# Seven-product matmuls with a 192-row first half: where the 64 leftover rows go

## The chip, the cores and the metric

The kernel runs on one core of a Trainium2 chip. The metric is the device time of one launch in microseconds (us); lower is better. A core has a matrix engine (PE, with its weight loads shown apart as PEld), a vector engine (DVE), a scalar engine (ACT), GpSimd (POOL) and SyncE (SP). Each engine works through its own queue in order. PE writes to PSUM, in banks of 512 float32 columns; DVE and ACT read it there. DMAs are issued from the queues of SP, POOL and ACT.

## The reference: two attention and two gated layers over 2048 tokens

The input is 2048 tokens of 448 features, in float32. The same two blocks are applied twice, with the same weights:

```python
x = x + attention(layernorm(x), wqkv, wo)      # 16 heads of 28
x = x + gated(layernorm(x), w_gate, w_up, w_down)
x = x + attention(layernorm(x), wqkv, wo)
x = x + gated(layernorm(x), w_gate, w_up, w_down)
# gated(z) = (sigmoid(z @ w_gate) * (z @ w_up)) @ w_down, inner size 1792
```

Gate, up, query, key and value products all sum over the 448 features. That sum is what the change rearranges: 448 is three times 128 and 64 more.

## The kernel before: seven products in place of eight, in float16 parts

**Number format.** A float32 operand is held as two float16 parts, high and low, with value = high + low. A product takes three matmuls: high x high, high weights x low input, low weights x high input. For the last 64 feature rows, two of these share one matmul of 128 rows: the lower 64 rows of an operand hold the part that the second product needs.

**Seven products.** Gate and up (from block to block of 512 tokens), and query and key in layer 1, are made two output tiles of 128 columns at a time. The features are cut into two halves, the tokens of a block into two halves of 256, and the output into the two tiles, so that one 2x2 by 2x2 block product of this kind would need eight products. The kernel uses a scheme with seven, on sums and differences of the halves. The first half of the features has 256 rows, the second 192 (128 and 64). Of the seven products, four (`k` = 0 to 3, input tile `wide`) involve 256 rows: two groups of 128 rows with three matmuls each, six matmuls. Three (`k` = 4 to 6, input tile `short`) involve 192 rows: three matmuls for the full group and two for the 64 rows, five matmuls. All are in `of_halves`, line 636 of the profile.

**Weights.** The sums and differences of the weights do not depend on the tokens. They are made once, during the attention of layer 0, by `Prepare`: its steps are tied to the key blocks that PE has mixed, one split of a tile pair about every nine key blocks. POOL's queue reads the raw weights ahead and writes the results back (lines 1365, 1367, 1388); DVE forms four sums (line 260), the high halves (line 266) and the low halves (line 269, `low` in `split_sums`). A pair's result has 25 groups of 128 columns (`N_SUMS`) and goes to DRAM. There are 14 gate and up splits and 3 for query and key. In the gated layers a pair's two tiles (gate and up) are loaded from there two pairs ahead, through POOL's queue (line 1744).

**Attention of layer 0.** For each head, PE makes scores in groups of three tiles (line 1503), ACT takes their exponentials (line 1518), PE mixes the values with them (line 1554). Two score tiles of most heads go aside: DVE makes their exponentials by a polynomial (lines 1528 to 1537). The aside scores go to the PSUM bank in which the head before was accumulated; DVE's transposition (line 1583, in `finish`) frees it. So DVE's queue holds, in program order: polynomial, the end of each head, and the splits of `Prepare`.

**Inputs.** `Block.half_steps` makes `wide` and `short` for a block of tokens, one step after another between the products of the block before: DVE subtracts, ACT writes the high halves (line 458), DVE the low ones (line 467). `raw` holds the features of a block as four groups; the fourth has only 64 rows, and its lower 64 rows are zeroed by POOL (line 477 in step `r11`). Three `double` copies and one copy of the remainder by ACT (lines 471 and 523) fill the lower 64 rows of `short` in the last steps.

**One pair of the gated stage.** `gate_and_up` issues for gate and up in turn: `first`, `apart`, `second`, `third` (the `wide` products), `c11_c22`, `c21`, `c12` (the `short` ones). `first`, `second` and `third` accumulate in one bank, which ACT copies out after each (line 1936), before the next may write it; DVE adds the side bank (lines 1952, 1959). From block 1 on, pieces of the down product of the block before stand between them (line 1863).

Of the kernel before, what the change touches and what calls it, by code (L numbers as in the profile page):

```python
# [19 lines left out]
P = 128  # L20
# [36 lines left out]
N_SUMS = 25  # L57
# [5 lines left out]
SHORT = ((10, 23, 12), (11, 24, 13), (8, 22, 9))  # L63
# [61 lines left out]
def interleaved_layers(ctx: ExitStack, tc: tile.TileContext, x_in, wqkv, wo, w_gate, w_up,  # L125
# [137 lines left out]
    def split_sums(t, v, by):  # L263
# [13 lines left out]
        for to, hi, a in ((t[:, 14:16], t[:, 0:2], v[:, 0:2, 0]),  # L277
                          (t[:, 16:20], t[:, 2:6], s12),
                          (t[:, 20:23], t[:, 6:9], s34[:, 0:3]),
                          (t[:, 23:25], t[:, 10:12], v[:, 2])):  # L280
            low(to, hi, a)
        low(t[64:P, 9], t[0:64, 9], s34[0:64, 3])
        low(t[64:P, 12:14], t[0:64, 12:14], v[0:64, 3])
# [23 lines left out]
    class Block:  # L307
# [91 lines left out]
        def gather(self):  # L399
            rows = self.scr.rearrange("j r i n -> (j r) (i n)")  # L400
            self.raw = big.get("xraw", [P, 4, W])
            nc.sync.dma_start(self.raw[:, 0:3, :],
                              rows[0:384].rearrange("(k p) n -> p k n", p=P))
            nc.sync.dma_start(self.raw[0:64, 3, :], rows[384:D])
# [25 lines left out]
        def half_steps(self):  # L430
# [38 lines left out]
            def double(to):  # L469

                nc.scalar.copy(to[64:P, 0, 1], to[0:64, 0, 1])


            def r11():
                self.wide = big.get("xwide", [P, 4, 2, 2, W // 2], F16)
                if not self.turned:
                    nc.gpsimd.memset(self.raw[64:P, 3, :], 0.0)
# [8 lines left out]
            def t2():  # L486
                low(self.wide[:, 1], self.t1)
                self.t3 = subtract("t3", cut(2, 2), cut(0, 2))
                high(self.wide[:, 2], self.t2)
                qrt.put(self.t1)  # L490

            def t3():
                low(self.wide[:, 2], self.t2)
                self.t4 = subtract("t4", cut(2, 0), self.t2)
                high(self.wide[:, 3], self.t3)
                qrt.put(self.t2)

            def r21():
                self.short = big.get("xshort", [P, 4 if self.whole else 3, 2, 2, W // 2], F16)
                low(self.wide[:, 3], self.t3)  # L500
                high(self.short[:, 0], cut(2, 0))
                qrt.put(self.t3)

            def t4():
                low(self.short[:, 0], cut(2, 0))
                high(self.short[:, 1], self.t4)

            def r22():
                low(self.short[:, 1], self.t4)
                double(self.short[:, 0])  # L510
# [7 lines left out]
            def last_low():  # L518
# [4 lines left out]
                nc.scalar.copy(self.short[64:P, 1, 1, 1], self.raw[64:P, 3, 0:W // 2])  # L523
                double(self.short[:, 1])
                big.put(self.raw)

            def last_rows():
                double(self.short[:, 2])
# [39 lines left out]
        def turn_raw(self):  # L568
# [3 lines left out]
            nc.gpsimd.memset(self.raw[64:P, 3, :], 0.0)  # L572
            for j in range(TB):
                self.turn(j)
            for kt, pt in self.pt.items():
                n = P if kt < 3 else 64
                nc.scalar.copy(self.raw[0:n, kt, :], pt[0:n])
# [45 lines left out]
    def of_halves(pm, w, blk, k, first):  # L623


        if k < 4:
            x = blk.wide[:, k]
            terms = [(w[:, i], x[:, j, t]) for t in range(2)
                     for i, j in ((2 * k + t, 0), (2 * k + t, 1), (14 + 2 * k + t, 0))]
# [1605 lines left out]
```

## Time and profile before

| what | value |
|---|---|
| median of 3 runs | 1886.36 us (1886.18 to 1886.47) |
| span of the profiled execution | 1884.5 us |
| end-to-end time of that execution | not listed apart; its span is 1.9 us below the median |
| first attention, exponentials of layer 0 | from about 120 to 560 us |
| gated stage of layer 0 | 599 to 952 us |
| query, key and value products of layer 1 | 952 to 1040 us |
| gated stage of layer 1 | 1528 to 1881 us |
| granted PE clock | 1.00 |
| DMA | 275.82 MB, mean 146 GB/s |

A row of the groups names the line, the engine, the operation and the tiles (result <- inputs), the shape, how often it ran, and its time. In a row in order of time, the first number is the start in us from the span's begin, the second the length; a bracket tells how long the engine was idle before it and what released it. A row that stands for several instructions ends in x and their count, and its length goes from the first start to the last end.

### The profile page before, as it was taken

What the parts mean: (1) busy time and instruction counts of PE and PEld (TensorE: products, weight loads), DVE (VectorE), ACT (ScalarE), POOL (GpSimd) and SP (SyncE); (2) the same over time, 40 slices, a digit from 0 to 9 for tenths busy, and PEclk for the clock granted to TensorE, in tenths of its full rate; (3) what the DMA queues carried; (4) which work ended last, traced back from release to release, by engine and by line L of the source; (5) the groups of instructions that cost most, each with busy time, mean ns of one, the idle gap of its engine ahead of it and who ended that gap; (6) DMA issues with size and microseconds to landing.
All of it is one profiled execution on the core that took longest, in us unless ns stands there. A gap on an engine that the chain in (4) does not pass through costs nothing. (4 is left out here: it accounts for less than half of the span.)

```text
span 1884.5 us, 57358 instructions
## 1 busy us (share of the span) xinstructions
PE 1875.9 (100%) x24609; PEld 1385.2 (74%) x24609; DVE 1489.2 (79%) x3018; ACT 1424.8 (76%) x1897; POOL 233.1 (12%) x458
## 2 busy tenths in 40 slices
PE   9999999999999999999999999999999999999999
PEld 4455555555566899999987566777876568999998
DVE  7758999998997887788877587787778689877664
ACT  6569999999993655555568899999999757555541
POOL 3001112222202111111110000000000021111110
PEclk9999999999999999999999999999999999999999
DMA  7674454454333755646763322122121246566553
GB/s 257 183 216 126 132 159 125 129 149 119 124 107 88 267 199 212 221 189 247 235 170 99 91 52 52 29 51 52 32 47 32 72 163 230 198 228 224 203 206 142
DMA packets 116005, 275.82 MB, mean 146 GB/s; under 512 B 14174, under 2 KB 72014, under 8 KB 115616
## 3 DMA queue, kind: packets, MB, share of 16 engines
q0 software_dynamic: 31952, 163.16, 24.1%
q1 hardware_dynamic: 82640, 107.55, 20.2%
q8 instruction: 195, 3.19, 0.7%
q10 hardware_dynamic: 1152, 1.38, 0.3%
q14 instruction: 66, 0.54, 0.1%
HBM read 210.57 MB, written 53.08 MB: 140 GB/s over the span
## 5 line engine op out<-in xcount | busy, mean ns | idle before, releaser
L1518 ACT ACTIVATE prob_s<-sc 128x1536 f32<-128x1536 f32 (+1 forms) x657 | 887.9, 1486 | 6.6 <-PE sc L1503 3.4
L1554 PE MATMUL acc<-prob_s,val_s 128*32 128x256 f32 (+3 forms) x7708 | 577.3, 383 | 0.0
L1503 PE MATMUL sc<-qp_s 114*32 114x512 f16 x7868 | 560.9, 379 | 0.0
L636 PEld LDWEIGHTS <-gu_s 128*128 128x128 f16 x4368 | 426.7, 98 | 45.9 <-PE op L1683 0.7
L1503 PEld LDWEIGHTS <-qp_s 114*32 114x32 f16 x8192 | 289.6, 96 | 187.9 <-issue 81.9
L1554 PEld LDWEIGHTS acc<-prob_s,val_s 128*32 128x32 f32 x7708 | 290.3, 110 | 125.9 <-issue 11.7
L636 PE MATMUL chain<-xwide_s,gu_s 128*128 128x256 f16 x2016 | 247.5, 273 | 0.0
L1863 PE MATMUL dnp<-dn_s,hparts_s 128*128 128x224 f16 x2184 | 245.9, 259 | 0.0
L1863 PEld LDWEIGHTS <-hparts_s 128*128 128x128 f16 x2184 | 210.2, 98 | 5.1
L1534 DVE SCALAR_TENSOR_TENSOR power_q<-power_q,expo_q 128x512 f32<-128x512 f32 x243 | 168.2, 692 | 8.3
L1936 ACT COPY one_q<-chain 128x256 f32<-128x256 f32 x224 | 82.3, 372 | 114.3 <-PE chain L636 113.8
L1952 DVE TENSOR_TENSOR one_q<-side,one_q 128x512 f32<-128x512 f32 x112 | 72.1, 686 | 97.7 <-PE side L636 97.5
L636 PE MATMUL side<-xshort_s,gu_s 128*128 128x256 f16 x1120 | 140.6, 273 | 0.0
L1744 POOL DMA_DIRECT2D gu_s<-gu_parts x104 | 55.9, 538 | 438.7 <-PE side L636 435.5
L1816 ACT CAST hparts_s<-hsums_q 128x256 f16<-128x256 f32 (+1 forms) x152 | 71.5, 485 | 35.8 <-DVE hsums_q L1828 23.4
L1554 PE MATMUL acc<-power_q,val_s 128*32 128x256 f32 (+3 forms) x300 | 94.2, 396 | 0.0
L636 PE MATMUL side<-xwide_s,gu_s 128*128 128x256 f16 x672 | 91.7, 273 | 0.0
L1583 DVE STREAM_TRANSPOSE oturned_q<-acc 128x512 f32<-128x512 f32 x32 | 22.9, 717 | 82.5 <-PE acc L1554 82.2
L1963 ACT ACTIVATE one_q<-one_q 128x512 f32<-128x512 f32 x56 | 35.3, 630 | 65.0 <-DVE one_q L1952 64.7
L1820 DVE TENSOR_TENSOR hparts_s<-hsums_q,hparts_s 128x256 f16<-128x256 f32 (+1 forms) x152 | 72.8, 517 | 5.7 <-ACT hparts_s L1816 5.7
L1528 DVE TENSOR_SCALAR expo_q<-aside,base 128x512 f32<-128x512 f32 x81 | 60.6, 748 | 21.0 <-PE aside L1503 20.6
L621 PE MATMUL qkp<-xhl_s,wqk_s 128*128 128x512 f16 x308 | 69.6, 379 | 0.9 <-ACT wqk_s L241 0.6
(258 smaller groups left out, 2410.2 us busy)
## 6 DMA issues: line engine op xcount, KB each, us to landing
gu_s<-gu_parts POOLq DMA_DIRECT2D x104, 800.0 KB, 5.9
dn_s<-dn_parts POOLq DMA_DIRECT2D x42, 784.0 KB, 7.5
qp_s<-qk_scr SPq DMA_DIRECT2D x96, 224.0 KB
gu_parts<-pack_s POOLq DMA_DIRECT2D x14, 800.0 KB, 3.8
xt_scr<-xs_s SPq DMA_DIRECT2D x48, 224.0 KB
xraw_s<-xt_scr SPq DMA_DIRECT2D x12, 768.0 KB
qk_scr<-qkhl_q SPq DMA_DIRECT2D x28, 256.0 KB
qp_s<-qk_scr SPq DMA_DIRECT2D x64, 112.0 KB
```

Source lines behind the costliest of these rows:

```text
L621: nc.tensor.matmul(pm, w, x, start=(i == 0), stop=(i == len(terms) - 1))
L636: nc.tensor.matmul(pm, a, x, start=(first and i == 0), stop=(i == len(terms) - 1), skip_group_check=True)
L1503: nc.tensor.matmul(ps[32 * j:32 * j + 32, :], hd.k[:, keys], hd.q[:, qb * W:(qb + 1) * W], start=True, stop=True, tile_position=(0, 32 * j))
L1518: nc.scalar.activation(prob[:, 0:n, :], ps[:, 0:n, :], AF.Exp, scale=exp_scale)
L1528: nc.vector.tensor_scalar(y, ps, base2[:, 0:1], -126.0, op0=ALU.mult, op1=ALU.max)
L1534: nc.vector.scalar_tensor_tensor(p, p, c[k], y, op0=ALU.add, op1=ALU.mult)
L1554: nc.tensor.matmul(acc[qb * VC:(qb + 1) * VC, s], v[:, kc % TB, h, :], probs[c * NB + qb][:, s], start=(kc == 0 and a == 0), stop=(kc == N ...
L1816: nc.scalar.copy(to[:, :, 0], a)
L1820: nc.vector.tensor_tensor(to[:, :, 1], a, to[:, :, 0], op=ALU.subtract)
L1863: nc.tensor.matmul(pm, a[:, x, t], w[:, p, y], start=(begin and n == 0 and (j == 0 or alone)), stop=(n == 2), skip_group_check=True)
L1936: nc.scalar.copy(to, pm)
L1952: nc.vector.tensor_tensor(one[m], side[m], one[m], op=ALU.add)
```

## The change: 192 rows first, and the 64 rows spread

The features change places: group 0 keeps rows 0 to 127, group 1 is now the 64 rows 384 to 447, groups 2 and 3 are rows 128 to 383 (`PLACES`). So the first half has 192 rows and the second 256. In the seven-product scheme the four `wide` products now have three matmuls for a full group and two for the 64 rows (`TAILS`), five matmuls; the three `short` products have two full groups, six matmuls.

Which lower rows hold what changes with it. `again` copies the high part of the 64 rows to the lower rows of the low part, in all four `wide` products (and, in layer 1, in the fourth `short` tile); `double` and the copy of the remainder go. In `last_rows`, DVE adds the lower rows of one `short` low part to those of another, and ACT copies them to the lower rows of the second `wide` tile. The zeroed lower rows are now in group 1.

The weights get 27 groups per pair. In `split_sums` the low halves are cut otherwise (five of 128 rows, three of 64 instead of four and two), POOL makes two copies, and DVE adds one group to another. POOL reads the raw weights in three DMAs per tile instead of two, and a block's `gather` on SP has three DMAs instead of two where the block is halved.

```diff
-N_SUMS = 25
+N_SUMS = 27
+PLACES = 0, 3, 1, 2
-SHORT = ((10, 23, 12), (11, 24, 13), (8, 22, 9))
+LOW_A = 14, 15, 16, 17
+TAILS = 1, 24, 25, 26
+SHORT = ((10, 12, 20, 22), (11, 13, 21, 23), (8, 9, 18, 19))
...
 # split_sums
-        for to, hi, a in ((t[:, 14:16], t[:, 0:2], v[:, 0:2, 0]),
-                          (t[:, 16:20], t[:, 2:6], s12),
-                          (t[:, 20:23], t[:, 6:9], s34[:, 0:3]),
-                          (t[:, 23:25], t[:, 10:12], v[:, 2])):
+        for to, hi, a in ((t[:, 14], t[:, 0], v[:, 0, 0]),
+                          (t[:, 15:17], t[:, 2:6:2], s12[:, 0:4:2]),
+                          (t[:, 17:19], t[:, 6:10:2], s34[:, 0:4:2]),
+                          (t[:, 19], t[:, 9], s34[:, 3]),
+                          (t[:, 20:24].rearrange("p (k z) n -> p k z n", k=2),
+                           t[:, 10:14].rearrange("p (k z) n -> p k z n", k=2), v[:, 2:4])):
             low(to, hi, a)
-        low(t[64:P, 9], t[0:64, 9], s34[0:64, 3])
-        low(t[64:P, 12:14], t[0:64, 12:14], v[0:64, 3])
+        low(t[64:P, 24:26], t[0:64, 3:6:2], s12[0:64, 1:4:2])
+        low(t[64:P, 26], t[0:64, 7], s34[0:64, 1])
+        low(t[64:P, 1], t[0:64, 1], v[0:64, 1, 0])
+        nc.gpsimd.tensor_copy(t[0:64, 24:27], t[0:64, 3:8:2])
+        nc.gpsimd.tensor_copy(t[64:P, 7], t[64:P, 23])
+        nc.vector.tensor_tensor(t[64:P, 19], t[64:P, 19], t[64:P, 23], op=ALU.add)
...
 # half_steps
-            def double(to):
-                nc.scalar.copy(to[64:P, 0, 1], to[0:64, 0, 1])
+            def again(to):
+                nc.scalar.copy(to[64:P, 1, 1], to[0:64, 0, 1])
             def r11():
                 self.wide = big.get("xwide", [P, 4, 2, 2, W // 2], F16)
                 if not self.turned:
-                    nc.gpsimd.memset(self.raw[64:P, 3, :], 0.0)
+                    nc.gpsimd.memset(self.raw[64:P, 1, :], 0.0)
                 self.t1 = subtract("t1", cut(0, 2), cut(0, 0))
                 high(self.wide[:, 0], cut(0, 0))
...
             def last_rows():
-                double(self.short[:, 2])
+                if self.whole:
+                    again(self.short[:, 3])
+                rows, lo = self.short[64:P, 1, 1, 1], self.short[64:P, 2, 1, 1]
+                nc.vector.tensor_tensor(rows, rows, lo, op=ALU.add)
+                nc.scalar.copy(self.wide[64:P, 1, 0, 1], lo)
...
 # of_halves
         if k < 4:
             x = blk.wide[:, k]
-            terms = [(w[:, i], x[:, j, t]) for t in range(2)
-                     for i, j in ((2 * k + t, 0), (2 * k + t, 1), (14 + 2 * k + t, 0))]
+            terms = [(w[:, 2 * k], x[:, 0, 0]), (w[:, 2 * k], x[:, 1, 0]),
+                     (w[:, LOW_A[k]], x[:, 0, 0]),
+                     (w[:, 2 * k + 1], x[:, 0, 1]), (w[:, TAILS[k]], x[:, 1, 1])]
         else:
             x = blk.short[:, k - 4]
-            main, low, tail = SHORT[k - 4]
-            terms = [(w[:, main], x[:, 0, 0]), (w[:, main], x[:, 1, 0]), (w[:, low], x[:, 0, 0]),
-                     (w[:, tail], x[:, 0, 1]), (w[:, tail], x[:, 1, 1])]
+            terms = [(w[:, SHORT[k - 4][i]], x[:, j, t])
+                     for t in range(2) for i, j in ((t, 0), (t, 1), (2 + t, 0))]
...
 # Prepare.read
-                    nc.gpsimd.dma_start(v[:, 0:3, z],
-                                        w[0:384, c].rearrange("(s p) n -> p s n", p=P))
-                    nc.gpsimd.dma_start(v[0:64, 3, z], w[384:448, c])
-                nc.gpsimd.memset(v[64:P, 3], 0.0)
+                    nc.gpsimd.dma_start(v[:, 0, z], w[0:P, c])
+                    nc.gpsimd.dma_start(v[:, 2:4, z],
+                                        w[P:384, c].rearrange("(s p) n -> p s n", p=P))
+                    nc.gpsimd.dma_start(v[0:64, 1, z], w[384:448, c])
+                nc.gpsimd.memset(v[64:P, 1], 0.0)
```

The products of the values, the lone query and key tile and the transposed copies follow the new places without a change of their count.

More of the change, by code (lines that the diff above doesn't have):

```diff
@@ L401, in gather @@
             self.raw = big.get("xraw", [P, 4, W])
-            nc.sync.dma_start(self.raw[:, 0:3, :],
-                              rows[0:384].rearrange("(k p) n -> p k n", p=P))
-            nc.sync.dma_start(self.raw[0:64, 3, :], rows[384:D])
+            tail = 1 if self.halves else 3
+            if self.halves:
+                nc.sync.dma_start(self.raw[:, 0, :], rows[0:P])
+                nc.sync.dma_start(self.raw[:, 2:4, :],
+                                  rows[P:384].rearrange("(k p) n -> p k n", p=P))
+            else:
+                nc.sync.dma_start(self.raw[:, 0:3, :],
+                                  rows[0:384].rearrange("(k p) n -> p k n", p=P))
+            nc.sync.dma_start(self.raw[0:64, tail, :], rows[384:D])
         def part(self, kt):
@@ L489, in t2 @@
                 high(self.wide[:, 2], self.t2)
+                again(self.wide[:, 0])
                 qrt.put(self.t1)
@@ L495, in t3 @@
                 high(self.wide[:, 3], self.t3)
+                again(self.wide[:, 1])
                 qrt.put(self.t2)
@@ L501, in r21 @@
                 high(self.short[:, 0], cut(2, 0))
+                again(self.wide[:, 2])
                 qrt.put(self.t3)
@@ L506, in t4 @@
                 high(self.short[:, 1], self.t4)
+                again(self.wide[:, 3])
             def r22():
                 low(self.short[:, 1], self.t4)
-                double(self.short[:, 0])
                 high(self.short[:, 2], cut(2, 2))
@@ L571, in turn_raw @@
             self.raw = big.get("xraw", [P, 4, W])
-            nc.gpsimd.memset(self.raw[64:P, 3, :], 0.0)
+            nc.gpsimd.memset(self.raw[64:P, 1, :], 0.0)
             for j in range(TB):
                 self.turn(j)
-            for kt, pt in self.pt.items():
+            for i, kt in enumerate(PLACES):
                 n = P if kt < 3 else 64
-                nc.scalar.copy(self.raw[0:n, kt, :], pt[0:n])
+                nc.scalar.copy(self.raw[0:n, i, :], self.pt[kt][0:n])
             big.put(self.xn)
```

20 lines of the change are left out of this document (9 added, 11 removed).

## The prediction

> **What bounds the kernel now.** I read the page first, then the busy time by stretch, the products' line, the order in time inside one pair, and the waits. On the page TensorE (PE) is busy all the way and nothing else is:
>
> ```profile
> span 1884.5 us, 57358 instructions
> PE 1875.9 (100%) x24609; PEld 1385.2 (74%) x24609; DVE 1489.2 (79%) x3018; ACT 1424.8 (76%) x1897; POOL 233.1 (12%) x458
> ```
>
> Pipelined matmuls hide short waits in such a figure, so the stages are read apart. Columns: stretch, length, busy us (and count) of PE, PEld, DVE, ACT, POOL, the granted clock, DMA share, GB/s.
>
> ```profile
> 258.00:549.00 291.00, 290.73 (x5320) 170.72 (x5312) 276.23 (x547) 290.82 (x217) 62.84 (x107) 1.00 0.44 129
> 668.00:952.00 284.00, 284.00 (x2737) 265.38 (x2735) 225.31 (x505) 156.22 (x375) 48.71 (x104) 1.00 0.61 218
> 1528.00:1852.00 324.00, 324.00 (x3032) 294.56 (x3029) 245.82 (x548) 180.54 (x447) 47.17 (x93) 1.00 0.58 209
> ```
>
> In the gated stages (the two lower rows) PE alone is full: DVE has 76 to 79% and ACT 55%. In the first attention (upper row) three engines are full: PE, ACT, and DVE with 276.2 of 291 us. There DVE prepares the weights between its other duties, and that is where this change adds work.
>
> **Gain: one matmul in 39.** A set of seven products is 4x6 + 3x5 = 39 matmuls; after, 4x5 + 3x6 = 38.
>
> ```profile
> L636 PEld LDWEIGHTS <-gu_s x4368: 95/98/98, 599.4 to 1850.9; 128*128 128x128 f16 x199
> L636 PEld LDWEIGHTS <-wsums_s x468: 95/98/98, 951.5 to 1031.3; 128*128 128x128 f16 x156
> 702.28 1.47 PE L636 MATMUL chain<-xwide_s,gu_s 128*128 128x256 f16 x12
> 703.59 0.82 PE L636 MATMUL side<-xwide_s,gu_s 128*128 128x256 f16 x6
> ```
>
> 4368/39 = 112 gate and up sets, 468/39 = 12 query and key sets. Twelve matmuls take 703.59 - 702.28 = 1.31 us, 0.109 us each. Gain: 112 x 0.109 = 12.2 us in the gated stages and 12 x 0.109 = 1.3 us in the projection.
>
> Does PE find its inputs earlier too? The tightest place is block 0, with no down pieces between the products:
>
> ```profile
> 647.78 1.26 PE L636 MATMUL side<-xshort_s,gu_s 128*128 128x256 f16 x10
> 648.59 1.29 DVE L1952 TENSOR_TENSOR one_q<-side,one_q 128x512 f32<-128x512 f32 x2 [0.33 <-PE side L636]
> 652.62 0.63 ACT L1936 COPY one_q<-chain 128x256 f32<-128x256 f32 x2
> 653.03 1.47 PE L636 MATMUL chain<-xwide_s,gu_s 128*128 128x256 f16 x12
> ```
>
> `second` (653.03) may write the bank only after ACT's copy, whose first half ends at 652.62 + 0.37 = 652.99. That copy hangs on a chain of DVE and ACT which began when `c11_c22(0)` ended. Between the two PE now has 43 matmuls, after the change 45 (the shorter products lie behind, the longer ones ahead), so this slack grows by 0.2 us. The next one, to `third`, goes from 61 matmuls to 60 and loses 0.1 us of about as much. I charge 0.3 us for all pairs of both layers.
>
> The copies to the lower rows: four `again` replace three `double` and one copy of the remainder, as many 0.4 us ACT copies, two steps later than what they read. One DVE add of 64x256 per block comes on top, hidden by the DVE's idle fifth. Gathers grow by one issue on SP, with nothing close behind it there; weight loads grow by 27/25. A pair's tiles are issued when the pair two ahead ends, so they have a whole pair (78 x 0.109 = 8.5 us in block 0) and take:
>
> ```profile
> gu_s<-gu_parts POOLq DMA_DIRECT2D x104, 800.0 KB, 5.9
> ```
>
> 6.4 us after: hidden by the pair between.
>
> **A wait that is added.** The zeroed lower rows move from the last quarter to the second, which the first step `r11` reads. POOL's memset, until now needed several steps later, becomes its input. Where it stands late:
>
> ```profile
> 956.37 0.52 POOL L477 MEMSET xraw_s<- 64x512 f32 x1
> 954.29 0.73 DVE L448 TENSOR_TENSOR t_q<-xraw_s 128x256 f32<-128x256 f32 x2
> 955.37 0.71 ACT L456 CAST xwide_s<-xraw_s 128x256 f16<-128x256 f32 x2
> 957.68 1.29 DVE L951 TENSOR_TENSOR one_q<-side,one_q 128x512 f32<-128x512 f32 x2 [0.33 <-PE side L636]
> ```
>
> DVE would start at 956.9 instead of 954.3 and ACT 1.5 us late; behind them stand the copies of the chain bank and L951, for which `c12` (at 959.04) waits. An input more can't gain; between 0 (absorbed) and the DVE's 2.6 us I take 1.2, near the ACT delay, less a little slack of PE.
>
> **Loss: the split of the weights.** 17 splits run in the first attention (14 gate and up, 3 query and key). DVE's part of one, low halves:
>
> ```profile
> 481.57 0.48 DVE L269 SCALAR_TENSOR_TENSOR pack_s<-raws_s,up,pack_s 128x256 f16<-128x256 f32 x1
> 481.96 1.27 DVE L269 SCALAR_TENSOR_TENSOR pack_s<-sums_q,up,pack_s 128x512 f16<-128x512 f32 x2
> 483.16 0.47 DVE L269 SCALAR_TENSOR_TENSOR pack_s<-raws_s,up,pack_s 128x256 f16<-128x256 f32 x1
> 483.65 0.34 DVE L269 SCALAR_TENSOR_TENSOR pack_s<-sums_q,up,pack_s 64x128 f16<-64x128 f32 x1
> 483.92 0.47 DVE L269 SCALAR_TENSOR_TENSOR pack_s<-raws_s,up,pack_s 64x256 f16<-64x256 f32 x1
> ```
>
> By start to start, 128 columns cost 0.27 us, 256 cost 0.39, 384 and 512 together 1.20 (0.53 and 0.66), and the change to the lower rows 0.10: 2.74 us with the last. After: 0.27, 0.39, 0.39, 0.27, 0.66, then 0.10, 0.39, 0.27, 0.27 and a 16-bit add of 128 columns, about 0.13: 3.14 us. **+0.40 us per split**, on the full engine.
>
> POOL gets two copies (three blocks of 128 columns, and one) and two more DMA issues per split. What POOL and DVE do to each other:
>
> ```profile
> L1588 DVE CAST ohl_q<-oraw_q x32: 426/428/633, 153.0 to 1496.6; 128x512 f16<-128x512 f32 x32
> 486.93 0.61 DVE L1588 CAST ohl_q<-oraw_q 128x512 f16<-128x512 f32 x1
> 486.52 0.77 POOL L1365 DMA_DIRECT2D raws_s<-in_B_w_gate_dram  x1
> L349 POOL TENSOR_SCALAR off<-off x20: 221/228/652, 589.4 to 1685.4; 128x2 f32<-128x2 f32 x20
> 612.30 0.69 DVE L229 TENSOR_TENSOR hhl_q<-two_q,hhl_q 128x512 f16<-128x512 f32 x1 [1.04 <-ACT hhl_q L228]
> 612.46 0.61 POOL L349 TENSOR_SCALAR off<-off 128x2 f32<-128x2 f32 x1
> L207 POOL CAST ind<-ind_f_q x1: 289/289/289, 10.8 to 10.8; 128x128 bf16<-128x128 f32 x1
> L1368 POOL MEMSET raws_s<- x17: 306/333/335, 238.3 to 515.7; 64x256 f32 x17
> ```
>
> A DVE cast beside a POOL issue takes 0.18 us more (0.61 against 0.43); a tiny POOL operation beside a two-input DVE one takes 0.61 instead of 0.23, it waited until DVE was through. So they exclude one another, and either can lose. The two issues more I price at 0.08 us of DVE per split (half of the 0.18, not each burst meets a cast). The copies: 0.29 us for 128 columns (L207) and, between the memsets of 256 (0.33) and 512 columns (0.52), 0.43 for 384, together 0.72. They meet DVE's low halves, which have two inputs. DVE loses between 0 (POOL always waits) and 0.72 (it waits out both). I take 0.25: without the 0.22 that L349 needs for two columns, 0.28 is left for the moving of data, and a little of it falls between DVE's instructions. Behind the copies in POOL's queue stand only the next split's write and reads, a whole split away. Together 0.40 + 0.08 + 0.25 = **0.73 us per split**, ends 0.40 and 1.20.
>
> The Trainium skill (SBUF — State Buffer, section "SBUF: two separate sides") speaks against the change here: DVE with two SBUF inputs and a POOL operation that reads SBUF share an exclusive port lock held for the whole instruction, and the loser fully blocks. The rows of L349 and L1588 agree that one blocks; by the rule's full length the price is the upper end.
>
> Does that reach PE? DVE's only idle time from 258 to 549 us is this:
>
> ```profile
> DVE oturned_q L1583 <- PE acc L1554: 4.2, 1, 4.2
> DVE expo_q L1528 <- PE aside L1503: 1.1, 2, 0.7
> ```
>
> And PE depends on DVE twice per aside block: its scores need the bank which L1583 frees, and the mix needs the powers of L1537.
>
> ```profile
> 374.21 0.72 DVE L1583 STREAM_TRANSPOSE oturned_q<-acc 128x512 f32<-128x512 f32 x1
> 375.13 0.40 PE L1503 MATMUL aside<-qp_s 114*32 114x512 f16 x4
> 361.56 0.69 DVE L1537 SCALAR_TENSOR_TENSOR power_q<-power_q,whole_q 128x512 f32<-128x512 f32 x1
> 363.03 0.59 PE L1554 MATMUL acc<-power_q,val_s 128*32 128x512 f32 x1
> 430.74 0.40 PE L1503 MATMUL aside<-qp_s 114*32 114x512 f16 x4 [0.27 <-DVE oturned_q L1583]
> 432.33 1.46 ACT L1518 ACTIVATE prob_s<-sc 128x1536 f32<-128x1536 f32 x1 [0.16 <-PE sc L1503]
> ```
>
> Slack is 0.20 us at 375, 0.78 at 363, and at 430 there is none: PE waits and ACT behind it. I replayed DVE's queue: same order and spacing, each split longer by x, its PE inputs moved by the delay so far, PE delayed where a release comes late. Almost nothing is absorbed: the 4.2 us of idle time lies behind most of the tight places. Seven aside blocks then make PE wait (at x = 0.73: 0.4 us near 264, then 1.7 near 363, 1.4, 1.1 and 1.9 up to 431, 2.0 near 514, 2.1 near 542), and the delay is 5.4 us for x = 0.40, 10.6 for 0.73, 18.1 for 1.20 (17 splits of x, less 1 to 2 us taken up). At 430 PE's 0.27 us cost ACT 0.16, so PE is ahead by some 0.1 at each place, 0.5 in all: **10.1 us**.
>
> **Sum.** -12.2 - 1.3 + 0.3 + 1.2 + 10.1 = -1.9 us. The profiled span, 1884.5 us, lies 1.9 below the median of 1886.36, taken as constant: **1884.5 us**.
>
> **Rivals.**
> - The copies cost DVE next to nothing (x = 0.48): delay 6.1, sum -5.9, 1880.5 us. For it: L349 shows POOL as the loser. Against: L1588 shows DVE as one.
> - Slower: each copy holds DVE for its whole length (x = 1.20): delay 17.6, sum +5.6, 1892.0 us. It breaks even at x = 0.85 and is slower by 0.2% from 1.09.
> - (By the lock of the Trainium skill's page it would be this last one.)
> - DVE waits inside a split: its closing add of the lower rows is held until POOL's copies are done, about 0.8 us for two of them and signals: x near 1.5, 1897 us. Against: the add touches other columns than the copies write.
> - DVE's lateness is taken up and the matmuls alone count: -12.0, 1874.4 us. Against: 276 of 291 us.
>
> **Chances.** Forecast 0.38, cheap copies 0.29, whole length 0.22, wait inside 0.06, absorbed 0.05. About 0.2% (3.8 us) is what counts as a change here. The forecast's own range is 1882 to 1887 (x from 0.6 to 0.88). Faster: 0.29 and 0.05 and a little of the first, 0.37; slower: most of 0.22, and 0.06, 0.28; same: 0.35. Range 1877 to 1894: it leaves out the absorbed case and the wait inside.
>
> **What would show it.** LDWEIGHTS at the products' line: 4256 and 456. Gated stages shorter by 6 us each. First attention, from its first to its last exponentials, longer by about 10 us, with PE waits at the aside scores on L1583 and late powers; DVE without its 4.2 us idle. Low halves of a split at 3.1 us without POOL, longer where copies overlap. At the first projection of layer 1, DVE and ACT waiting for the memset. It would be wrong if the attention kept its length (absorbed), or if the splits grew by over a microsecond.

## The result: 8 us slower, and the profile after

The changed kernel takes 1894.51 us (median; 1894.36 to 1896.08), the kernel before 1886.41 us on the same chip: a ratio of 1.0044, 95% interval 1.003 to 1.0058. The forecast was 1884.5 us, 1.9 us faster than before, with a range from 1877 to 1894: the kernel became slower, and its time lies above the range. The profiled execution has a span of 1892.9 us, 8.4 us longer than the one of before.

The page of the changed kernel, its head (busy time, share of the span, instructions of each engine), and then the busy time by stretch, with the columns as in the prediction; the stretches are those of before, moved to where the same work now lies:

```profile
span 1892.9 us, 57291 instructions
PE 1869.3 (99%) x24485; PEld 1396.0 (74%) x24485; DVE 1512.9 (80%) x3081; ACT 1431.1 (76%) x1913; POOL 267.5 (14%) x526
```

```profile
258.00:562.00 304.00, 294.35 (x5320) 180.76 (x5319) 289.85 (x598) 292.49 (x217) 96.68 (x173) 0.99 0.43 127
680.80:960.60 279.80, 279.66 (x2690) 260.83 (x2689) 228.65 (x506) 157.76 (x381) 49.08 (x103) 1.00 0.64 232
1542.00:1860.80 318.80, 318.18 (x2973) 289.03 (x2972) 250.11 (x553) 179.82 (x448) 47.44 (x93) 1.00 0.61 223
```

The upper row is the first attention. The same 5320 matmuls and 217 exponentials now stretch over 304 us instead of 291; PE is no longer full (294.35 of 304), and neither is ACT. DVE is busy 289.85 us where it was 276.23, with 51 instructions more. The two lower rows, the gated stages, are 4 to 5 us shorter. PE's waits, most costly first, with total, times and the longest:

```profile
PE aside L1524 <- DVE oturned_q L1604: 8.6, 6, 2.6
PE chain L656 <- ACT one_q L955: 2.7, 3, 1.4
PE chain L656 <- ACT val_s L1109: 2.1, 1, 2.1
PE still L314 <- DVE warm L190: 1.3, 1, 1.3
PE side L656 <- DVE one_q L1973: 1.1, 2, 0.6
PE aside L1524 <- DVE expo_q L1549: 1.1, 1, 1.1
```

Before, the first row stood at 0.3 us, the second was absent, and of the fifth there was nothing. (Lines have moved: L1524 is the scores' L1503, L1604 the transpose L1583, L656 the products' L636, L955 the bank copy L935, L1973 the sum L1952.) By stages, from the first and last row of the exponentials and of the products in each trace:

| stage (us) | before | after | difference | forecast |
|---|---|---|---|---|
| first attention, first to last exponential | 444.3 | 457.3 | +12.9 | +10.1 |
| gated, layer 0, first to last product | 322.8 | 318.5 | -4.2 | -6 |
| projection, layer 1, first product to first exponential | 96.6 | 101.4 | +4.8 | -0.1 |
| second attention | 443.6 | 443.6 | 0 | 0 |
| gated, layer 1 | 322.8 | 317.9 | -4.9 | -6 |
| all the rest | 254.4 | 254.2 | -0.2 | 0 |
| span | 1884.5 | 1892.9 | +8.4 | -1.9 |

So three terms were too small at once: 2.8 us in the attention, 4.9 in the projection, 2.8 in the gated stages, together 10.5 us. With 0.2 us less in the rest, these are the 10.3 us between the forecast and the measured change of the span.

**The attention.** DVE's low halves of one split in the changed kernel, and POOL beside them:

```profile
490.65 0.59 DVE L272 SCALAR_TENSOR_TENSOR pack_s<-raws_s,up,pack_s 128x128 f16<-128x128 f32 x1
491.16 1.13 DVE L272 SCALAR_TENSOR_TENSOR pack_s<-sums_q,up,pack_s 128x256 f16<-128x256 f32 x3
492.22 0.74 DVE L272 SCALAR_TENSOR_TENSOR pack_s<-raws_s,up,pack_s 128x512 f16<-128x512 f32 x1
492.99 0.86 DVE L272 SCALAR_TENSOR_TENSOR pack_s<-sums_q,up,pack_s 64x256 f16<-64x256 f32 x2
493.77 0.34 DVE L272 SCALAR_TENSOR_TENSOR pack_s<-raws_s,up,pack_s 64x128 f16<-64x128 f32 x1
494.14 0.22 DVE L292 TENSOR_TENSOR pack_s<-pack_s 64x128 f16<-64x128 f16 x1
494.40 0.72 DVE L1604 STREAM_TRANSPOSE oturned_q<-acc 128x512 f32<-128x512 f32 x1
```

```profile
490.40 0.69 POOL L290 COPY pack_s<-pack_s 64x384 f16<-64x384 f16 x1 [10.45 <-DVE pack_s L269]
493.02 0.29 POOL L291 COPY pack_s<-pack_s 64x128 f16<-64x128 f16 x1 [1.93 <-DVE pack_s L272]
```

From 490.65 to DVE's next work at 494.40 are 3.75 us; before it was 2.85 (the prediction's split, from 481.57 to the next start at 484.42). That is x = 0.90 us per split, not 0.73, and nearly every later split shows the same 3.75.

**The projection.** The zeroing, and who waited for it:

```profile
963.94 0.27 POOL L345 TENSOR_SCALAR rs<-mv 128x2 f32<-128x2 f32 x1 [1.57 <-DVE mv L342]
...
965.66 0.52 POOL L491 MEMSET xraw_s<- 64x512 f32 x1
```

```profile
966.21 0.41 ACT L471 CAST xwide_s<-xraw_s 128x256 f16<-128x256 f32 x1 [1.72 <-POOL xraw_s L491]
...
968.61 0.63 ACT L916 ACTIVATE qkhl_q<-one_q 128x512 f16<-128x512 f32 x1 [0.93 <-DVE one_q L971]
```

```profile
966.21 0.42 DVE L463 TENSOR_TENSOR t_q<-xraw_s 128x256 f32<-128x256 f32 x1 [2.06 <-POOL xraw_s L491]
```

That is the wait that was forecast. PE itself loses little of it here (0.34 and 0.22 us at 966.94 and 968.63). The larger loss comes 20 and 50 us later:

```profile
987.82 1.25 PE L656 MATMUL chain<-xwide_s,wsums_s 128*128 128x256 f16 x10 [2.06 <-ACT val_s L1109]
989.41 0.71 PE L656 MATMUL side<-xwide_s,wsums_s 128*128 128x256 f16 x5 [0.34 <-ACT val_s L1109]
991.17 1.25 PE L656 MATMUL chain<-xwide_s,wsums_s 128*128 128x256 f16 x10 [1.06 <-ACT one_q L955]
```

and 1.35 us more for the same bank copy at 1016.75. In ACT's queue, three copies `again` (L486) stand between the value copies and ahead of the bank copy that PE waits for:

```profile
986.79 0.40 ACT L486 COPY xwide_s<-xwide_s 64x256 f16<-64x256 f16 x1
987.22 0.54 ACT L1109 ACTIVATE val_s<-vp 128x448 f32<-128x448 f32 x1
...
988.39 0.40 ACT L486 COPY xwide_s<-xwide_s 64x256 f16<-64x256 f16 x1
988.82 0.54 ACT L1109 ACTIVATE val_s<-vp 128x448 f32<-128x448 f32 x1
...
989.89 0.40 ACT L486 COPY xwide_s<-xwide_s 64x256 f16<-64x256 f16 x1
990.32 0.54 ACT L1109 ACTIVATE val_s<-vp 128x448 f32<-128x448 f32 x1
990.76 0.64 ACT L955 COPY one_q<-chain 128x256 f32<-128x256 f32 x2
```

In the kernel before, the value copies follow one another more closely, and the first copy to the lower rows (`double`, L471) stands behind the bank copy (L935):

```profile
975.63 0.53 ACT L1089 ACTIVATE val_s<-vp 128x448 f32<-128x448 f32 x1
...
976.66 0.54 ACT L1089 ACTIVATE val_s<-vp 128x448 f32<-128x448 f32 x1
...
977.61 0.55 ACT L1089 ACTIVATE val_s<-vp 128x448 f32<-128x448 f32 x1
978.04 0.65 ACT L935 COPY one_q<-chain 128x256 f32<-128x256 f32 x2
978.72 0.40 ACT L471 COPY xshort_s<-xshort_s 64x256 f16<-64x256 f16 x1
```

Two causes were to be told apart: the late zeroing, and the copies `again`.

**The gated stages.** From pair to pair the first products start exactly 0.22 us earlier, the two matmuls a pair (2 x 0.109), in 42 of the 54 steps. The others lie in four places: the first pair of each layer is 0.50 us longer, where PE waits 0.56 us for the sum L1973; in block 0 the pairs 4 to 6 (counted from 0) take 8.41, 8.52 and 8.39 us instead of 8.30; the first pair of block 1 gains 0.13 us in layer 1 and loses 0.23 in layer 0; and two pairs of block 3 in layer 0 gain 0.11 and 0.01.

### The profile page after: what moved, and what is told of

Same layout as the page of the kernel before. It is cut to its first block, busy times and chain, and to the rows that moved or that the text cites. A ratio compares the mean times of both kernels' runs of the same rounds, so it can differ in the third digit from the quotient of the medians.

```text
span 1892.9 us, 57291 instructions
## 1 busy us (share of the span) xinstructions
PE 1869.3 (99%) x24485; PEld 1396.0 (74%) x24485; DVE 1512.9 (80%) x3081; ACT 1431.1 (76%) x1913; POOL 267.5 (14%) x526
## 5 line engine op out<-in xcount | busy, mean ns | idle before, releaser
L1575 PE MATMUL acc<-prob_s,val_s 128*32 128x256 f32 (+3 forms) x7708 | 584.2, 384 | 0.0
L1524 PE MATMUL sc<-qp_s 114*32 114x512 f16 x7868 | 568.4, 380 | 0.0
L656 PEld LDWEIGHTS <-gu_s 128*128 128x128 f16 x4256 | 415.7, 98 | 47.7 <-issue 2.6
L1524 PEld LDWEIGHTS <-qp_s 114*32 114x32 f16 x8192 | 301.9, 96 | 189.1 <-issue 82.4
L1575 PEld LDWEIGHTS acc<-prob_s,val_s 128*32 128x32 f32 x7708 | 303.1, 110 | 111.8 <-issue 10.8
L656 PE MATMUL chain<-xwide_s,gu_s 128*128 128x256 f16 x1680 | 210.8, 273 | 0.3
L656 PE MATMUL side<-xshort_s,gu_s 128*128 128x256 f16 x1344 | 165.0, 273 | 1.1 <-DVE one_q L1973 1.1
L1973 DVE TENSOR_TENSOR one_q<-side,one_q 128x512 f32<-128x512 f32 x112 | 74.9, 690 | 71.7 <-PE side L656 71.4
L1604 DVE STREAM_TRANSPOSE oturned_q<-acc 128x512 f32<-128x512 f32 x32 | 22.9, 717 | 81.1 <-PE acc L1575 80.8
L656 PE MATMUL chain<-xshort_s,gu_s 128*128 128x256 f16 x672 | 82.5, 273 | 0.0
L656 PE MATMUL side<-xwide_s,gu_s 128*128 128x256 f16 x560 | 79.4, 273 | 0.0
```

What stands on the lines that cost most here:

```text
L656: nc.tensor.matmul(pm, a, x, start=(first and i == 0), stop=(i == len(terms) - 1), skip_group_check=True)
L1524: nc.tensor.matmul(ps[32 * j:32 * j + 32, :], hd.k[:, keys], hd.q[:, qb * W:(qb + 1) * W], start=True, stop=True, tile_position=(0, 32 * j))
L1575: nc.tensor.matmul(acc[qb * VC:(qb + 1) * VC, s], v[:, kc % TB, h, :], probs[c * NB + qb][:, s], start=(kc == 0 and a == 0), stop=(kc == N ...
L1973: nc.vector.tensor_tensor(one[m], side[m], one[m], op=ALU.add)
```

## The experiments

The profiles give each stage's length; whole times of the variants spread by 2 to 5 us between runs of one kernel, so single stages carry the readings.

One thing disturbs even these. Right behind some of PE's longest waits, the traces show a stretch of 3.4 us in which the granted clock was 0.50. The changed kernel's trace has one from 525.7 to 529.1 us, behind PE's wait of 2.57 us that ended at 524.81. It leaves the 12.9 us as they are: 1.6 us are lost there, and PE's wait near 557 us is 1.7 us shorter than in e2 (below), which has no such stretch in its first attention and the same length, 457.2 us.

### The attention: DVE's work alone, and without POOL's copies

**e6_before_low_twice**, the kernel before with more DVE work and nothing else:

```diff
                           (t[:, 16:20], t[:, 2:6], s12),
+                          (t[:, 16:20], t[:, 2:6], s12),
                           (t[:, 20:23], t[:, 6:9], s34[:, 0:3]),
```

> The kernel before with one low half of each split done twice (four blocks of 128 columns, 0.66 us of DVE, same result): DVE work alone, no POOL copy and no other edit. Replay of DVE's queue: each 1 us added to all 17 splits costs 16 us, less 1.55: the first attention is longer by 16 x 0.66 - 1.55 = 9.0 us (444.3 to 453.3), the kernel by 9.0 us; no other stage moves. Rival (DVE's lateness is mostly taken up, and the lengthening by 12.9 us in the changed kernel has another source, POOL or DMA): under 4 us.

Measured: 1895.57 us (before 1886.59), first attention 454.0 us, +9.7; the split's low halves take 3.52 us, 0.67 more. The other stages keep their lengths (the projection, 0.6 us shorter, moves most). PE's waits:

```profile
PE aside L1504 <- DVE oturned_q L1584: 7.6, 6, 2.2
...
PE aside L1504 <- DVE expo_q L1529: 0.9, 1, 0.9
```

DVE work alone, without any of the change's other edits, makes PE wait at the same place and in the same number of blocks.

**e4_rows_by_dma**, the changed kernel without POOL's copies:

```diff
-        nc.gpsimd.tensor_copy(t[0:64, 24:27], t[0:64, 3:8:2])
-        nc.gpsimd.tensor_copy(t[64:P, 7], t[64:P, 23])
...
-                nc.gpsimd.dma_start(*self.pack)
+                    nc.gpsimd.dma_start(to[:, 8:24], t[:, 8:24])
+                    nc.sync.dma_start(to[:, 0:7], t[:, 0:7])
+                    nc.sync.dma_start(to[0:64, 7], t[0:64, 7])
+                    nc.sync.dma_start(to[64:P, 7], t[64:P, 23])
+                    nc.sync.dma_start(to[0:64, 24:27], t[0:64, 3:8:2])
+                    nc.sync.dma_start(to[64:P, 24:27], t[64:P, 24:27])
```

> The changed kernel without the two POOL copies per split: the rows they copied are written straight from where they stand in the pack, by DMAs of SP (five more per split; POOL's own write stays one issue). Theory (POOL's copies stretch DVE's low halves, 0.24 and 0.12 us, and the rest of the added 0.9 us is DVE's own added work): a split's low halves and add fall from 3.75 to about 3.3 us, DVE is longer by about 0.5 us per split than before the change instead of 0.9, and the first attention goes from 457.3 to 451.0 us (16 x 0.5 - 1.55 = 6.5 us over before's 444.3); kernel 6 us faster. Rival (the two copies cost DVE nothing and the 0.9 us are its own instructions): first attention stays above 456 us. If the added DMA issues on SP hold up the stores and loads of the heads, new waits for operands show on PE.

Measured: 1890.50 us, first attention 452.0, 5.3 us below the changed kernel. The split without the copies:

```profile
487.03 0.35 DVE L272 SCALAR_TENSOR_TENSOR pack_s<-raws_s,up,pack_s 128x128 f16<-128x128 f32 x1
487.29 1.14 DVE L272 SCALAR_TENSOR_TENSOR pack_s<-sums_q,up,pack_s 128x256 f16<-128x256 f32 x3
488.35 0.75 DVE L272 SCALAR_TENSOR_TENSOR pack_s<-raws_s,up,pack_s 128x512 f16<-128x512 f32 x1
489.13 0.74 DVE L272 SCALAR_TENSOR_TENSOR pack_s<-sums_q,up,pack_s 64x256 f16<-64x256 f32 x2
489.79 0.34 DVE L272 SCALAR_TENSOR_TENSOR pack_s<-raws_s,up,pack_s 64x128 f16<-64x128 f32 x1
490.16 0.22 DVE L290 TENSOR_TENSOR pack_s<-pack_s 64x128 f16<-64x128 f16 x1
490.42 0.72 DVE L1611 STREAM_TRANSPOSE oturned_q<-acc 128x512 f32<-128x512 f32 x1
```

3.39 us here and 3.38 in most splits, so DVE's own added work is 0.53 us, and the copies cost it 0.37: the first low half needs 0.26 us to the next start instead of 0.51, the two of 64 rows 0.66 instead of 0.78. The copies' price is shown; so is that they are the smaller part of the 0.90.

**e5_add_on_pool**, e4 and the closing add moved:

```diff
-        nc.vector.tensor_tensor(t[64:P, 19], t[64:P, 19], t[64:P, 23], op=ALU.add)
+        nc.gpsimd.tensor_tensor(t[64:P, 19], t[64:P, 19], t[64:P, 23], op=ALU.add)
```

> As e4_rows_by_dma (rows written straight by DMA, no POOL copies), and the closing add of 64 rows by 128 columns of each split on POOL instead of DVE. Theory (the first attention is longer by about 14.5 us for each us that DVE spends more on each of the 17 splits, whatever the work is): DVE's part falls by the add's 0.26 us from 3.38 to 3.12 us, or to 3.3 if POOL's add stretches a low half beside it as the copy did; the first attention goes from 452.0 (e4) to 448.3, at the worst 451; the kernel from 1890.5 to about 1887, level with before. Rival (the add on DVE was hidden, the rest of the lengthening is the new lower halves alone): first attention within 0.7 us of 452.0.

Measured: 1888.63 us, first attention 450.0. The split takes 3.31 us, the upper of the two values given: DVE no longer does the add's 0.26, but the two low halves beside POOL's add take 0.84 us to the next start instead of 0.66.

The four attentions against DVE's time per split, and the replay's line 16x - 1.55 (the prediction's 16x - 1.05 less the 0.5 us of PE's lead):

| kernel | x | longer by | 16x - 1.55 |
|---|---|---|---|
| e5_add_on_pool | 0.46 | 5.7 | 5.8 |
| e4_rows_by_dma | 0.53 | 7.7 | 6.9 |
| e6_before_low_twice | 0.67 | 9.7 | 9.2 |
| changed kernel | 0.90 | 12.9 | 12.9 |

Whatever lengthens DVE, its own instructions or a copy beside them, the attention follows it by the same line.

### The attention: relief for DVE elsewhere

**e13_after_fewer_asides** and **e11_before_fewer_asides** give two blocks of exponentials, one each in heads 10 and 14, back from DVE to ACT, in the changed kernel and in the one before:

```diff
-FEW = "2222222222222223"
+FEW = "2222222222122213"
```

> The changed kernel as it stands, only with one block of exponentials in each of heads 10 and 14 given back to ACT. Theory (the loss in the first attention is lateness of DVE which nothing takes up; two reliefs of some 6.4 us take up what has gathered in the heads before and after them): first attention from 457.3 to between 450 and 453 us, kernel 1888.5 (level with before to 0.1%). By the waits at 432 and 544 alone (2.2 and 0.8 us), less 1.0 us for ACT: 455.2. Rival (POOL's copies or DMA hold up PE in another way than through DVE): no change, or 1 us longer as ACT pays.

> The kernel before with the same two blocks given back to ACT: the counterpart without the change's work on DVE. Theory (before the change DVE's lateness costs almost nothing, so relief buys little and ACT's two thirds of an exponential are paid): first attention longer by 0.6 to 1.0 us, kernel 1887.3. Rival (DVE held up the attention before, too): first attention shorter by 1 us or more.

Measured: the changed kernel falls to 1885.94 us (before 1886.62 on the same chip, ratio 0.9995, interval 0.9986 to 1.0004), its first attention from 457.3 to 448.3 us. The kernel before stays at 1886.62 (ratio 0.9999), its attention 444.7 instead of 444.3. These lengths go from start to start, and with both edits the last exponential has 1536 columns where it had 512, so that its start lies 0.9 us farther ahead of the end of the stage. To the end of the last exponential, the changed kernel's attention is 8.1 us shorter and that of the kernel before 1.2 us longer. So DVE held up the changed kernel and not the one before. The relief of 8.1 us was larger than the waits at its two places; the lateness that these heads would have handed on is gone as well. PE's waits in e13, from 238 to 575 us, are 3.1 us in all, where the changed kernel has 9.7:

```profile
PE aside L1524 <- DVE oturned_q L1604: 2.0, 3, 1.3
PE aside L1524 <- DVE expo_q L1549: 1.1, 1, 1.1
```

### The projection and the first pair

**e1_memset_ahead** moves the zeroing to the place where the buffer is handed out:

```diff
             if self.halves:
+                nc.gpsimd.memset(self.raw[64:P, 1, :], 0.0)
                 nc.sync.dma_start(self.raw[:, 0, :], rows[0:P])
...
-                if not self.turned:
-                    nc.gpsimd.memset(self.raw[64:P, 1, :], 0.0)
```

> The changed kernel with the zeroing of the lower rows of the second quarter issued on POOL as soon as the quarter buffers are handed out (ahead of the gather's DMAs) instead of inside the step r11. Theory (the zeroing is late: DVE L463 waited 2.1 us and ACT L471 1.7 us for it, the query and key tiles came 1.2 us later, their stores with them, and the lifts and the bank copies queued behind): the projection of layer 1, from its first query/key product to the first exponential, falls from 101.4 to about 98.5 us, the PE wait of 2.1 us for val_s goes to under 0.7, and the kernel is about 3 us faster. Rival (the four copies of 64 rows per block, which stand earlier in ACT's queue than the copies they replace, make the later work late): the projection stays within 0.5 us of 101.4 us though the wait for the zeroing is gone. First attention and gated stages unchanged by both within 0.3 us.

Measured: projection 99.1 us, 2.3 us less; the wait for val_s falls from 2.1 to 0.9, those for the bank copies stay (2.4 us). The first attention of this run was 2.4 us longer, in two jumps where the edit does nothing: 1.5 us near 442 us, where the granted clock was 0.50 for 3.4 us behind a PE wait of 2.60 us, and 0.8 us near 136 us, whose cause is open. So the whole time (1895.74) says little.

**e2_again_on_pool** takes the four copies from ACT's queue:

```diff
             def again(to):
-                nc.scalar.copy(to[64:P, 1, 1], to[0:64, 0, 1])
+                nc.gpsimd.tensor_copy(to[64:P, 1, 1], to[0:64, 0, 1])
```

> The changed kernel with the four copies `again` of each block on POOL instead of ACT. Theory of the copies' place (ACT's queue): the PE waits for bank copies in the projection (1.06 us near 991 and 1.35 us near 1017) go, the projection falls by 2 us or more from 101.4 us; the first pair of gate and up of each layer loses its wait of 0.56 us for DVE L1973 (pair 9.02 us to about 8.5) and the gated stages are 0.5 us shorter each; kernel about 3 us faster. Theory of the zeroing alone: the projection changes by less than 0.7 us, since the wait for the zeroing near 966 is still there. It could also get longer, if the copies queue on POOL behind the norms' small operations.

Measured: projection 98.6 us, 2.8 less, with the waits for one_q down from 2.7 to 0.8; the first pair of each layer 8.31 us instead of 9.02, somewhat more than expected; pair 4 of block 0, in return, takes 0.5 us more in each layer. The kernel grew to 1897.38 us, and the stretch between gated stage and projection by 5.2 us. In that stretch, POOL's longest waits, and PE's:

```profile
POOL xshort_s L486 <- DVE xshort_s L479: 15.2, 1, 15.2
POOL dn_s L1778 <- PE side L656: 7.3, 1, 7.3
```

```profile
PE dnp L1884 <- DMA dn_s<-dn_parts: 3.5, 1, 3.5
```

A copy that waits on POOL holds up the weight loads behind it in POOL's queue. That is 3.5 of the 5.2 us. The rest is the clock: right behind PE's wait, which ended at 942.25, the granted clock (0.50 below) was halved for 3.4 us, half of which is 1.7 us.

```profile
942.70:946.10 3.40, 3.40 (x22) 2.76 (x20) 0.65 (x1) 1.04 (x3) 0.00 (x0) 0.50 0.63 256
```

**e7_projection** puts the two together, the copies on POOL only in the blocks where nothing stands behind them:

```diff
+                copy = nc.gpsimd.tensor_copy if self.by_pool else nc.scalar.copy
+                copy(to[64:P, 1, 1], to[0:64, 0, 1])
...
+        b2.by_pool = b3.by_pool = layer > 0
...
+        first.by_pool = True
```

> The changed kernel with the zeroing ahead (as e1) and the copies `again` on POOL only for the first block behind the attention and for the third and fourth block of the projection (the others stay on ACT, since with all on POOL the stretch between the gated stage and the projection grew by 5.2 us). Theory (zeroing and ACT's earlier copies each delayed the projection by about 2.5 us, independently): projection of layer 1 from 101.4 to about 96.5 us, the level of before; first pair of gate and up of each layer 8.3 us instead of 9.0, gated stages 0.7 us shorter each; stretch between gated stage and projection 29.5 as before; first attention unchanged (457.3); kernel about 6 us faster than the changed one, 1888. Rival (both edits remove the same wait): projection no lower than 98.3 us.

Measured: 1889.91 us; projection 97.5 us; first pairs 8.31 us; the stretch before the projection 29.6. The two edits bring 3.9 us together, less than the 5.1 of both alone: they share a part. Of PE's waits there remain 1.8 us for val_s and 0.5 for a bank copy. By the trace the value copies stand on ACT behind a lift which waits 2.4 us for a slot of a query or key tile whose store has not left yet; what sets the time of these stores was not tried.

### Everything together, and what was left

**e8_all** is e5 and e7 in one.

> e5 and e7 together: rows by DMA, add on POOL, zeroing ahead, chosen `again` copies on POOL. Theory (the three losses are independent, and behind them stands the gain of one matmul in 39): first attention 448.3, projection 96.5, gated stages 317.8 and 317.2: 8.5 us below the changed kernel in the attention plus 0.4 for the rest of it, 4.9 in the projection, 1.4 in the gated stages, span 1892.9 - 14.7 = about 1878, median about 1880: faster than before by 0.3%. Rival (with one loss gone another wait takes its place): above 1885.

Measured: 1883.26 us (before 1886.73; ratio 0.9981, interval 0.9972 to 0.9991): faster than both kernels, by less than expected. The attention is 449.9 and the projection 97.2 us, but between gated stage and projection 1.5 us have come up, and one pair of block 0 in layer 0 takes 0.8 us longer.

**e9_casts_behind** takes up the three pairs of block 0 that did not get shorter:

```diff
-                at[0].append(made.parts)
-                at[1].append(made.rest)
+                at[b == 0].append(made.parts)
+                at[1 + (b == 0)].append(made.rest)
```

> e8_all, and in block 0 of the gated stage the casts L1837 of a pair's operands stand behind the bank copies of `second` on ACT (they are issued one step later in block 0 only). Theory (the pairs 4 to 6 of block 0 did not get shorter by two matmuls, 8.41, 8.52 and 8.39 us instead of 8.30, because `third` waits 0.1 to 0.25 us for the copy of `second`, which is queued on ACT behind two of these casts): these three pairs take 8.30 to 8.32 us in both layers, 0.4 us less per layer, and the kernel 0.8 us less than e8, 1882.5. Rival (the loop over DVE's sums and the sigmoid bounds these pairs at 8.5 us): the three pairs stay as they are or another of them grows; kernel as e8 or slower.

Measured: 1882.71 us; the three pairs take 8.30, 8.39 and 8.41 us in layer 0 and 8.30, 8.39 and 8.30 in layer 1. Five of the six are shorter by about 0.1 us than in the changed kernel, together 0.57 of the 0.82 us that they had missed: the casts were most of it. The middle pair now waits in another place: its `second` starts at 657.95, just behind ACT's copy of `first` (657.54 to 657.90), and 0.21 us behind the matmul before it instead of 0.11.

**e10_fewer_asides** adds the relief of e13.

> e9, and one of the two blocks of exponentials that DVE makes by powers goes back to ACT in each of heads 10 and 14 of layer 0. Theory (DVE is what delays the attention at the places where PE waits for L1604, and what ACT has to take over costs only its own time, a third of 1.46 us each, 1.0 us in all): of the PE waits at 432 (1.4 us) and 544 (1.5 us) 2 us or more go, first attention 449.9 - 2.9 + 1.0 = 448.0; kernel 1.5 to 2 us below e9. Rival (another release takes over at these places, or the wait moves to the next aside): first attention 450 to 451.

Measured: 1877.23 us (ratio 0.9949, interval 0.9936 to 0.9963); first attention 445.5 us, 1.2 us over before's from start to start and 2.0 us to the end of the last exponential. The expected 448 was too cautious, for the same reason as in e13.

**e12_zero_late_blocks** keeps the early zeroing for the third and fourth block only:

```diff
-            if self.halves:
+            if self.halves and self.b > 1:
                 nc.gpsimd.memset(self.raw[64:P, 1, :], 0.0)
```

> e10, with the zeroing ahead only for the third and fourth block; the second block's stays in its step r11. Theory (with the zeroing of the second block ahead, POOL stood 13.1 us before it until the slot was free, the loads of down weights behind it in POOL's queue came late, and PE waited 1.7 us for dn_s in the stretch between gated stage and projection, 31.3 instead of 29.5 us): this stretch is 29.5 to 29.7 us again, nothing else moves, kernel 1.7 us below e10, 1875.5. Rival (the wait for dn_s comes from the rows that SP now writes, or from the shorter stages alone): the stretch stays at 31 us.

Measured: the stretch is 29.5 us again, and the one wait of PE that e10 had in it is gone:

```profile
PE dnp L1894 <- DMA dn_s<-dn_parts: 1.7, 1, 1.7
```

The kernel's time is the same, 1877.29 us (before 1886.62; ratio 0.995, interval 0.9936 to 0.9963), its span 1875.0 instead of 1875.5: the pair of block 0 that was 0.8 us too long in e8 is so again by 0.7, after 0.3 in e9 and nothing in e10. PE waits there for the second of the pair's two weight tiles, which landed 8.0 us after its issue in e8, 7.9 in e12 and 7.5 in e9, but after 6.5 us in e10 and 6.4 in the changed kernel. What makes this load slow is open.

## Why the prediction was wrong, step by step

- **The gain of one matmul in 39: right.** 4256 and 456 weight loads stand in the trace, and wherever nothing else binds a pair is 0.22 us shorter.
- **"I charge 0.3 us for all pairs": mis-sized, measured 3.1 us.** The slack before `second` and `third` was weighed in the steady pairs only, and one of its two places was judged rightly: in the changed kernel `third` waits up to 0.23 us for a bank copy, most of which e9 cured. The larger part, 0.72 us at each first pair (0.50 longer instead of 0.22 shorter), was in a place not looked at: DVE still finishes the block's own preparation there, and ACT's added copies make that late. e2 and e7 removed it.
- **"As many 0.4 us ACT copies, two steps later than what they read": this is the step that failed.** Their count was taken, not their place in ACT's queue. They stand before the bank copies and value copies that PE waits for, where the old ones stood behind. e2 puts 2.8 us of the projection on them (1.2 of these are shared with the zeroing, by e7), and the 0.72 us of each first pair.
- **The zeroing: right cause, priced 1.2 us, measured 2.3 us in e1.** The waits at the place itself were forecast (0 to 2.6 us). Missed was what is reached through other work: the query and key tiles leave 1.2 us later and, as the rows suggest, hold their slots that much longer, so that the lift on ACT and the value copies behind it come late (ACT's wait before the lift was 2.2 us and is 1.1 in e1). Little is lost at the place itself; PE pays 20 us later.
- **x = 0.73 per split: mis-sized, 0.90.** DVE's own part was put at 0.40 and is 0.53; the closing add, whose 0.13 no row had shown, took 0.26. The 0.08 for POOL's added issues fall outside the low halves and were not measured apart. The copies were put at 0.25 and cost 0.37. The rival with the whole length (1.20) was further off than the forecast. By the Trainium skill (SBUF — State Buffer, "SBUF: two separate sides") one of the two would block for the other's whole instruction. The trace agrees, and shows why the price is still less than the copy's length: the low half beside the larger copy ends 0.15 us after it (491.24 against 491.09) in 16 of the 17 splits, the one of 256 columns beside the smaller copy ends 0.27 us after that copy. The difference, 0.12 us, is what 128 more columns take. So the columns are worked off only once POOL is through, and what DVE loses is the overlap (0.44 and 0.32 us) less about 0.2 us that a low half needs anyhow ahead of its columns: 0.25 and 0.12. The add on POOL in e5 fits: overlap 0.37, loss 0.18.
- **The replay: right.** At the measured x it gives 12.9 us, and 12.9 were measured; three kernels with other x lie within 0.8 us of its line. "Almost nothing is absorbed" holds. One sign did not come: DVE was to lose its idle time of 4.2 us, and 3.3 us of it are left; the 0.9 us taken up there are one split's x.
- **The rivals.** None of them described what happened: the slower one came to +5.6 us by the splits alone. The splits cost 2.8 us more than forecast, and 7.7 us beyond the 1.5 priced came up in the projection and the gated stages, for which there was no rival. Of these, e7 takes back 3.9 and 1.3 us by the copies' place and the zeroing, and e9 0.6 by the casts' place; for the remaining 1.9 us no run shows the cause.

## What to carry to other kernels

When a change moves an operation earlier in an engine's queue, price what stands behind it, not the operation: four copies of 0.4 us, as many as before, cost over 4 us because bank copies for PE stood behind them. Follow a forecast wait to the resources that the late work holds, slots above all; it may come out far from where it arose. And where one engine is nearly full beside a bound one, replaying its queue with x more per step is a sound forecast, but small errors of x count as many times as there are steps (17 here); then look first for work to give to another engine: two blocks of exponentials, about 1 us of ACT, took back 8.1 of the 12.9 us.

## What the runs showed of the hardware

- A two-input DVE operation waits for a POOL copy or add that runs when it starts: it ended 0.15 us (128 columns) or 0.27 us (256) after POOL did, and lost the overlap less about 0.2 us. A POOL copy of 64x384 in 16 bits took 0.50 us at the shortest and 0.69 mostly; the DVE operation of 128 columns beside it took 0.51 us to the next start instead of 0.26. A POOL add of 64x128 took 0.71 us beside DVE, and cost DVE 0.18.
- A POOL instruction that waits for data holds up the DMAs issued behind it in its queue: a copy waiting 15.2 us in e2 and a zeroing waiting 13.1 us in e10 ended as PE waits of 3.5 and 1.7 us for weights.
- The closing add of 64x128 in 16 bits on DVE took 0.26 us from start to start where 0.13 was estimated, and the low half before it 0.37 instead of 0.27 (e4). That an instruction which needs the one before it starts later would fit both; so would the change between upper and lower rows, which costs 0.10 us at the first low half of 64 rows already. Neither was tested.
- Behind PE waits of 2.6 to 3.5 us the granted clock was 0.50 for 3.4 us in five places (the changed kernel at 525.7 us, e1 at 439.1 and 527.8, e7 at 526.1, e2 at 942.7). Behind waits of the same 2.6 us in e2 (ending at 438.6 and 524.7) it stayed 1.00, so the wait alone does not decide it.
